# A planned attention-plus-MLP kernel: a new order for the first batch, filler matmuls, one burst of key sums, free choice of buffer slots, and 15 squares on ScalarE

## The chip, the cores and the metric

The kernel runs on one core of a Trainium2 chip. The metric is the device time in microseconds (us). The span that the profile shows is from the first to the last instruction. A run over 1.5% above the fastest of the same kernel is called slow. A ratio is the mean time of one kernel's fast runs over that of the other's from the same rounds, so it is not quite the ratio of the medians that are quoted.

## The reference

```python
def phi(x):                                   # r = 8, so phi has 64 features
    a = einsum('rd,bhsd->bhsr', S1, x)
    b = einsum('rd,bhsd->bhsr', S2, x)
    return einsum('bhsi,bhsj->bhsij', a, b).reshape(..., 64)
q_p, k_p = phi(q), phi(k)                     # batch 4, heads 4, seq 1088, head_dim 32
kv  = einsum('bhsf,bhsd->bhfd', k_p, v)
z   = sum(k_p, axis=2)
x   = einsum('bhsf,bhfd->bhsd', q_p, kv) / (einsum('bhsf,bhf->bhs', q_p, z) + 1e-6)
x   = x.transpose(0, 2, 1, 3).reshape(4352, 128)
out = relu(x @ w_in)**2 @ w_out               # w_in 128 x 2048, w_out 2048 x 128
```

## The kernel before

The program first collects all operations with a planned duration on an engine, their dependencies and a priority, and then `Plan.run` lists them out in order of a simulated time. What the planner decides is the order of instructions on each engine and the slot of each buffer; each engine runs its list in order, and semaphores do the waiting. A batch has a **key** stage (k is transposed, projected to kab, transposed to ab; VectorE forms the 64 products kp; PE sums kv and z). A **unit** of 512 tokens has a query stage (qT, a sketch of 32 matmuls, a ScalarE copy bs, a VectorE product qp, den, its reciprocal, num, xT) and a **MoE** stage of eight tiles, each: two h matmuls, a relu on ScalarE, a square on VectorE, two o matmuls.

Buffers come back in the order in which they were taken:

```python
    for buf in op.take:                       # Plan.ready
        used, bufs = self.used[buf.pool], self.pools[buf.pool][3]
        if len(used) >= bufs:
            for d in used[len(used) - bufs].readers:
                ...
                t = max(t, d.end)
```

The loads of a batch go out as k, v, q, with q in one piece; the weights follow once batch 0's k is there:

```python
    k_ops = ...; v_ops = ...                  # k in two pieces, v in six
    q_op = dma("SP", lambda e: e.dma_start(out=qst.tile, in_=qb), deps=deps, prio=prio, take=[qst])
...
    nc.gpsimd.tensor_copy(gate, loaded[0][0].tile[:, 2 * C8 - 1 : 2 * C8])
    nc.gpsimd.dma_start(out=w_in_sb, in_=...)
    nc.gpsimd.dma_start(out=w_out_sb, in_=...)
```

A MoE tile, with the choice of the squaring engine (the list is empty before the change):

```python
    a2: nc.scalar.activation(rl.tile[:, :, :R], h.tile[:, :, :R], ACTF.Relu)
    alts = {"DVE": ... eng.tensor_mul(g.tile, rl.tile, rl.tile)}
    if i in SQ_ACT:                           # SQ_ACT = ()
        alts = {"ACT": ... eng.activation(g.tile, rl.tile, ACTF.Square)}
```

PSUM holds a ring of three two-bank slots (`ring`, for h, kab, the two sketch halves, the turned key sums, den and num), one bank for o and one for kv.

Of the kernel before, what the change touches and what calls it, by code (L numbers as in the profile page):

```python
# [36 lines left out]
class Plan:  # L37
# [3 lines left out]
    def __init__(self, pools):  # L41
        self.pools = pools
        self.ops = []
        self.used = {name: [] for name in pools}
# [9 lines left out]
    def ready(self, op):  # L54
        t = 0.0
        for d in op.deps:
            if d.end is None:
                return None
            t = max(t, d.end)
        for d in op.after:  # L60
            if d.issued is None:
                return None
            t = max(t, d.issued)
        for buf in op.take:
            used, bufs = self.used[buf.pool], self.pools[buf.pool][3]
            if len(used) >= bufs:
                for d in used[len(used) - bufs].readers:
                    if d.end is None:
                        return None
                    t = max(t, d.end)  # L70
        return t

    def run(self):
        free, mode, left, log = {}, {}, list(self.ops), []
        while left:
            best = {}
            for op in left:
                t = self.ready(op)
                if t is None:
                    continue  # L80
                for eng, (busy, lat, fn) in op.alts.items():
                    at = max(t, free.get(eng, 0.0))
                    best.setdefault(eng, []).append((at, op))
            assert best, "no operation is ready"
            eng = min(best, key=lambda e: min(a for a, _ in best[e]))
# [5 lines left out]
            busy, lat, fn = op.alts[eng]  # L91
            if op.mode is not None:
                if mode.get(eng, op.mode) != op.mode:
                    at += MODE_SWITCH
                mode[eng] = op.mode
            free[eng] = at + busy
            op.issued, op.end = at + busy, at + lat
            for buf in op.take:
                pool, shape, dtype, _ = self.pools[buf.pool]
                buf.tile = pool.tile(shape, dtype, tag=buf.pool, name=buf.name)  # L100
                self.used[buf.pool].append(buf)
# [6 lines left out]
SLACK = 0.05  # L108
MODE_SWITCH = 0.1
WARM = 12  # L110
KP_POOL = ()
SQ_ACT = ()
TOGETHER = True
K_LEAD = 18.0
Q_LEAD = 2.0
Q_END = 0.0
# [3 lines left out]
def kernel(  # L120
# [26 lines left out]
    def pool(name, shape, bufs, dtype=F32, space=None):  # L147
        if space is None:
            p = ctx.enter_context(tc.tile_pool(name=name, bufs=bufs))
        else:  # L150
            p = ctx.enter_context(tc.tile_pool(name=name, bufs=bufs, space=space))
# [5 lines left out]
    assert LEFT == 2  # L157

# [59 lines left out]
    def load(b, prio, deps=(), first="SP"):  # L218
# [6 lines left out]
        for i, (c0, c1) in enumerate(((0, 2 * C8), (2 * C8, S))):  # L225
            k_ops.append(dma(
                ("SP", first)[i],
# [3 lines left out]
                deps=deps, after=k_ops[:1], prio=prio, take=[kst] if i == 0 else [],  # L231
            ))
        v_ops = []
        for c in range(4):
# [6 lines left out]
                deps=deps, after=v_ops[:1], prio=prio, take=[vt] if c == 0 else [],  # L241
            ))
        for c in range(LEFT):
# [6 lines left out]
                deps=deps, after=v_ops[:1], prio=prio,  # L250
            ))
        q_op = dma(
            "SP", lambda e: e.dma_start(out=qst.tile, in_=qb),
            deps=deps, prio=prio, take=[qst],
        )
        loaded[b] = (kst, k_ops, vt, v_ops, qst, q_op)

    load(0, -90.0, first="ACT")
# [11 lines left out]
    w_op = plan.add("POOL", 3.0, 8.0, weights, deps=loaded[0][1], prio=-80.0)  # L270

    def warm():
        ps = Buf("o", "warm_ps")
        for n in range(WARM):
            plan.add(
                "PE", 0.43, 0.6,
                lambda: nc.tensor.matmul(  # L277
                    ps.tile, zeros[:, :128], zeros, start=True, stop=True
                ),
                prio=-100.0, take=[ps] if n == 0 else [], last=[ps], mode="full",  # L280
            )

    warm()

    def sketches():
# [17 lines left out]
        plan.add("SP", 0.0, 3.5, lambda: None, prio=-99.0)], prio=-95.0)  # L303
# [25 lines left out]
    def keys(b, prios):  # L329
        kst, k_ops, vt, v_ops, _, _ = loaded[b]  # L330
        kT, ab, kv, ps = Buf("kT", "kT"), Buf("ab", "ab"), Buf("kv", "kv_ps"), Buf("ring", "kab_ps")
        p = lambda x: prios[0] + x * (prios[1] - prios[0])
        tr = []
        for i, (c0, c1) in enumerate(((0, 2 * C8), (2 * C8, S))):
# [5 lines left out]
                deps=[k_ops[i]], after=tr[:1], prio=p(0.05 * i), take=[kT] if i == 0 else [], last=[kst],  # L340
# [4 lines left out]
        def project():  # L345
# [19 lines left out]
        pr = plan.add("PE", 1.0, 1.25, project, deps=tr + [sk_op], prio=p(0.1),  # L365
# [7 lines left out]
            deps=[pr], prio=p(0.15), take=[ab], last=[ps],  # L373
# [7 lines left out]
            deps=[pr], after=[main], prio=p(0.16), last=[ps],  # L381
        )

        def sums():
            nc.tensor.matmul(
                kv.tile[:, : F + H * r], zeros[:, :128], zeros[:, : F + H * r],
                start=True, stop=False, skip_group_check=True,
            )
            for t in range(T8 + 1):
# [10 lines left out]
        last = plan.add("PE", 0.6, 0.8, sums, deps=[main, tail], prio=p(0.2),  # L400
                        take=[kv], last=[ab], mode="k")
        zsum = last
        steps = [last]
        for x, (t0, t1) in enumerate(((0, 4), (4, T8), (T8, T8 + 1))):
# [4 lines left out]
            def product(eng, t0=t0, t1=t1, P=P, n=n, kp=kp):  # L409
# [8 lines left out]

            alts = {"DVE": ((1.12, 1.25) if n > 1 else (0.33, 0.45)) + (
                lambda product=product: product(nc.vector),)}  # L420
            if (b, x) in KP_POOL:
                alts = {"POOL": ((2.4, 2.6) if n > 1 else (0.8, 0.9)) + (
                    lambda product=product: product(nc.gpsimd),)}
            pd = plan.either(alts, deps=[main, tail], prio=p(0.25 + 0.2 * x),
                             take=[kp], last=[ab])

            def accumulate(t0=t0, t1=t1, P=P, kp=kp):
                for t in range(t0, t1):
                    for h in range(H):
# [9 lines left out]
            last = plan.add("PE", 0.12 * n, 0.12 * n + 0.25, accumulate,  # L439
                            deps=[pd] + v_ops, after=[last], prio=p(0.3 + 0.2 * x),  # L440
                            last=[kp, vt], mode="k")
            steps.append(last)
        kvT, zd, st = Buf("kvT", "kvT"), Buf("zd", "zd"), Buf("ring", "st_ps")
# [9 lines left out]
            deps=[zsum, mk_op], prio=p(0.76), take=[zd], last=[kv],  # L453
# [6 lines left out]
            deps=steps, prio=p(0.75), take=[kvT], last=[kv],  # L460
        )

        def turn():
            nc.tensor.matmul(
                st.tile[:, 1, : H * r],
                spread.rearrange("p c i j -> p (c i j)"),
                zd.tile.rearrange("p h j -> p (h j)"),
                start=True,
                stop=True,
            )  # L470
            nc.tensor.transpose(
                st.tile[:, 0, :128], kvT.tile.rearrange("p c f -> p (c f)"), ident
            )

        tn = plan.add("PE", 0.4, 0.6, turn, deps=[c1, d1], prio=p(0.8),
                      take=[st], last=[kvT, zd], mode="full")
# [4 lines left out]
                in0=st.tile[:, 1, : H * r].rearrange("p (h j) -> p h j", h=H),  # L481
# [3 lines left out]
            deps=[tn], prio=p(0.85), take=[zj], last=[st],  # L485
# [4 lines left out]
                kvs.tile[:, 0].rearrange("p h d -> p (h d)"), st.tile[:, 0, :128]  # L490
            ),
            deps=[tn], prio=p(0.85), take=[kvs], last=[st],
# [6 lines left out]
            deps=[d2], prio=p(0.9), take=[zc], last=[zj],  # L499
# [6 lines left out]
            deps=[d3, c2], prio=p(1.0), last=[zc],  # L506
        )
        state[b] = (kvs, [c2, d4])


    x_ready = {}

    def queries(u, prios):
# [4 lines left out]
        p = lambda x: prios[0] + x * (prios[1] - prios[0])  # L518
# [3 lines left out]
        while c0 < g0 + 2 * W:  # L522
# [7 lines left out]
                deps=[loaded[b][5]], after=tr[:1], prio=p(0.0), take=[qT] if not tr else [],  # L530
# [19 lines left out]
        if TOGETHER:  # L550
            op = plan.add("PE", 0.1 + 0.78 * f, 0.3 + 0.78 * f, lambda: sketch((0, 1)),
                          deps=tr + [sk_op], prio=p(0.15), take=ps, last=[qT], mode="q")
            sk = [op, op]
        else:
            sk = []
            for g in range(2):
                sk.append(plan.add(
                    "PE", 0.1 + 0.78 * f, 0.3 + 0.78 * f, lambda g=g: sketch((g,)),
                    deps=tr + [sk_op], prio=p(0.15 + 0.2 * g), take=[ps[g]], last=[qT],
                    mode="q"))  # L560
        prods = []
        for g in range(2):
# [6 lines left out]
                deps=[sk[g]], prio=p(0.2 + 0.2 * g), take=[bs], last=[ps[g]],  # L569
# [9 lines left out]
                deps=[cp], after=prods[:1], prio=p(0.3 + 0.2 * g), take=[qp] if g == 0 else [],  # L579
                last=[bs, ps[g]],  # L580
            ))
        dps, nps = Buf("ring", "den_ps"), Buf("ring", "num_ps")
        batches = sorted({g0 // S, (g0 + 2 * W - 1) // S})
        st_deps = [d for b in batches for d in state[b][1]]
        kvs_last = [state[b][0] for b in batches]

        def apply(x, to):
            for h in range(H):
                for c in range(2):
                    f0 = g0 + W * c  # L590
                    while f0 < g0 + W * c + W:
# [4 lines left out]
                            to.tile[32 * h : 32 * h + 32, c, w0 : w0 + f1 - f0],  # L596
# [7 lines left out]
        da = plan.add("PE", 0.05 + 0.42 * f, 0.28 + 0.42 * f, lambda: apply(1, dps),  # L604
                      deps=prods + st_deps, prio=p(0.55), take=[dps], last=[qp] + kvs_last,
                      mode="nd")
# [3 lines left out]
            lambda: nc.vector.transpose(dT.tile[:, :, :W], dps.tile[:, :, :W]),  # L610
            deps=[da], prio=p(0.6), take=[dT], last=[dps],
# [8 lines left out]
            deps=[t1], prio=p(0.65), take=[den], last=[dT],  # L620
# [4 lines left out]
            deps=[t2], prio=p(0.7), take=[rec], last=[den],  # L625
# [7 lines left out]
            deps=[t3], prio=p(0.75), take=[rT], last=[rec],  # L633
        )
        na = plan.add("PE", 0.05 + 0.42 * f, 0.28 + 0.42 * f, lambda: apply(0, nps),
                      deps=prods + st_deps, after=[t3], prio=p(0.8), take=[nps],
                      last=[qp] + kvs_last, mode="nd")
# [126 lines left out]
```

## Time and profile before

| | before |
|---|---|
| median time | 126.31 us (126.28 to 126.38, 3 runs) |
| the profiled run | 128.53 us, span 126.7, granted clock 0.929, slow |
| first relu begins | 26.18 us |
| first relu to end of last relu | 95.1 us |
| end of last relu to end of span | 5.4 us |

The profile's page of the kernel before: busy time by engine, and then the span in 40 slices of 3.17 us, each digit the busy share in tenths; PEclk is the granted clock of the matrix engine.

```profile
PE 110.2 (87%) x1378; PEld 50.5 (40%) x1396; DVE 105.1 (83%) x208; ACT 78.6 (62%) x99; POOL 3.3 (3%) x14
PE   6973785789999999999989979999899999999940
DVE  3445756889979999999989995999999899997940
ACT  3000313036848488589657766878898898899920
PEclk9999555557999999999999999999999999999998
```

There are two regimes. In the first nine slices no engine stays full, and the clock is at half in slices 5 to 9; from there on PE and VectorE (DVE) are near 9 everywhere. The windows view of the same kernel gives the numbers: us of the stretch, its length, then busy us (and instructions) of PE, PE's weight loads, DVE, ACT, POOL, then the clock, the DMA share and GB/s.

```profile
core 0: us, PE busy (x) PEld busy (x) DVE busy (x) ACT busy (x) POOL busy (x), PEclk, DMA share, GB/s
8.00:12.00 4.00, 1.17 (x37) 0.84 (x43) 2.03 (x4) 0.00 (x0) 0.08 (x1) 1.00 1.03 304
16.00:20.00 4.00, 3.45 (x50) 1.45 (x50) 1.54 (x6) 1.11 (x3) 0.00 (x0) 0.50 1.28 287
...
26.18:121.32 95.14, 91.57 (x1133) 42.41 (x1151) 89.10 (x173) 74.64 (x92) 0.00 (x0) 0.98 0.20 40
```

The timeline of the kernel before, lines from its start (start us, us, engine, line, operation, what stood before it in brackets):

```profile
10.81 0.71 DVE L527 STREAM_TRANSPOSE qT<-qst 128x512 f32<-128x512 f32 x1 [1.77 <-DMA qst<-in_q_dram]
11.44 2.64 DVE L412 TENSOR_TENSOR kp<-ab 128x1024 f32<-128x1024 f32 x3
17.12 2.01 PE L542 MATMUL qab_ps<-qT,S12q 32*64 32x256 f32 x32 [0.55 <-DVE zj L479]
25.13 0.59 PE L664 MATMUL h_ps<-xT,w_in_sb 128*128 128x512 bf16 x1 [0.91 <-DVE xT L640]
26.18 1.02 ACT L673 ACTIVATE rl<-h_ps 128x1024 bf16<-128x1024 f32 x1 [5.95 <-remote]
28.97 1.06 PE L692 MATMUL o_ps<-g,w_out_sb 128*128 128x512 bf16 x2
```

VectorE stands for q in its program order although the inputs of kp, next in its list, have been there for 1.8 us; a sketch takes 2.01 us at half clock, where later ones take 1.1. The chain of waits that ended last, by engine, and the DMA issue of w_out (KB, us to landing):

```profile
PE 53%; DVE 25%; ACT 7%; DMA 4%; issue 3%; SPq 3%; DVEq 0%; ACTq 0%
...
w_out_sb<-in_moe_w_out_dram POOLq DMA_DIRECT2D x1, 512.0 KB, 18.8
```

The w_out load was issued at 6.91 us and so landed at 25.7, three microseconds before it was used. Nothing waited for it.

### The profile page before, as it was taken

The numbers are of one execution on the slowest core, as the hardware profiler recorded it, in microseconds if no ns is written. First come the engines' busy times: TensorE is split into PE (matmuls) and PEld (weight loads), VectorE is DVE, ScalarE is ACT, GpSimd is POOL, SyncE is SP. The second block draws the span as 40 slices with busy tenths as digits, with TensorE's granted clock in tenths as the row PEclk, the third lists the DMA queues.
The fourth block names the chain that finished last, engine by engine and source line by source line (L and its number), as shares of the span: only waits on it lengthen the run. The fifth ranks groups of instructions, "written<-read, shape, count | busy, mean of one in ns | idle before, by whom it ended". The sixth has DMA issues, their size and how long they took to land.

```text
span 126.7 us, 3355 instructions
## 1 busy us (share of the span) xinstructions
PE 110.2 (87%) x1378; PEld 50.5 (40%) x1396; DVE 105.1 (83%) x208; ACT 78.6 (62%) x99; POOL 3.3 (3%) x14
## 2 busy tenths in 40 slices
PE   6973785789999999999989979999899999999940
PEld 2231541234544543534444434334445343434620
DVE  3445756889979999999989995999999899997940
ACT  3000313036848488589657766878898898899920
POOL 3050000000000000000000000000000000000000
PEclk9999555557999999999999999999999999999998
DMA  2999999950033263050003100220013050031042
GB/s 32 294 272 273 246 282 265 241 174 33 5 85 81 39 111 124 5 83 3 5 2 57 29 0 5 38 45 0 0 28 60 0 90 3 0 57 31 7 76 41
DMA packets 25871, 10.21 MB, mean 81 GB/s; under 512 B 22144, under 2 KB 24192, under 8 KB 25856
## 3 DMA queue, kind: packets, MB, share of 16 engines
q1 hardware_dynamic: 23360, 8.64, 29.6%
q0 software_dynamic: 2208, 1.05, 6.2%
q10 hardware_dynamic: 288, 0.31, 1.0%
q8 instruction: 11, 0.18, 0.6%
q14 instruction: 4, 0.03, 0.1%
HBM read 8.81 MB, written 2.23 MB: 87 GB/s over the span
## 4 chain that ended last, share of the span: by engine, by line
PE 53%; DVE 25%; ACT 7%; DMA 4%; issue 3%; SPq 3%; DVEq 0%; ACTq 0%
PE o_ps L692 17%; PE h_ps L664 16%; DVE g L682 7%; ACT rl L673 7%; PE qab_ps L542 7%; DVE kp L412 4%; DMA qst<-in_q_dram 4%; PE num_ps L595 4%; PE kv_ps L430 4%; PE den_ps L595 3%; DVE qp L573 3%; DVE qT L527 3%; DVE ot L702 2%; PE kab_ps L348 2%; SPq L237 1%
## 5 line engine op out<-in xcount | busy, mean ns | idle before, releaser
L673 ACT ACTIVATE rl<-h_ps 128x1024 bf16<-128x1024 f32 (+1 forms) x72 | 66.5, 980 | 21.8 <-PE h_ps L664 12.6
L682 DVE TENSOR_TENSOR g<-rl 128x1024 bf16<-128x1024 bf16 (+1 forms) x72 | 44.8, 642 | 3.3 <-ACT rl L673 3.1
L692 PE MATMUL o_ps<-g,w_out_sb 128*128 128x512 bf16 (+1 forms) x137 | 37.4, 371 | 1.9 <-DVE g L682 1.2
L664 PE MATMUL h_ps<-xT,w_in_sb 128*128 128x512 bf16 (+1 forms) x133 | 37.3, 373 | 1.8 <-DVE xT L640 0.9
L664 PEld LDWEIGHTS <-w_in_sb 128*128 128x128 bf16 x144 | 12.9, 98 | 18.6 <-issue 6.8
L692 PEld LDWEIGHTS <-w_out_sb 128*128 128x128 bf16 x144 | 13.1, 98 | 17.6 <-issue 7.7
L566 ACT COPY bs<-qab_ps 128x512 f32<-128x512 f32 (+1 forms) x18 | 9.2, 565 | 14.8 <-PE qab_ps L542 14.7
L542 PE MATMUL qab_ps<-qT,S12q 32*64 32x256 f32 (+1 forms) x288 | 12.4, 405 | 3.5 <-DVE qT L527 2.1
L573 DVE TENSOR_TENSOR qp<-qab_ps,bs 128x512 f32<-128x512 f32 (+1 forms) x18 | 11.3, 650 | 1.0 <-ACT bs L566 0.8
L412 DVE TENSOR_TENSOR kp<-ab 128x1024 f32<-128x1024 f32 (+1 forms) x12 | 10.8, 921 | 0.0
L542 PEld LDWEIGHTS qab_ps<-qT,S12q 32*64 32x64 f32 x288 | 6.2, 139 | 8.4 <-DVE qT L527 2.2
L595 PE MATMUL den_ps<-qp,kvs 64*32 64x256 f32 (+3 forms) x168 | 7.3, 391 | 1.7 <-DVE den L615 1.5
L610 DVE STREAM_TRANSPOSE dT<-den_ps 128x512 f32<-128x512 f32 (+1 forms) x9 | 6.1, 675 | 2.7 <-PE den_ps L595 2.7
L527 DVE STREAM_TRANSPOSE qT<-qst 128x512 f32<-128x512 f32 (+7 forms) x12 | 6.4, 533 | 2.0 <-DMA qst<-in_q_dram 1.8
L430 PE MATMUL kv_ps<-kp,vt 128*32 128x64 f32 (+1 forms) x288 | 7.2, 238 | 0.8 <-DVE kp L412 0.3
L430 PEld LDWEIGHTS kv_ps<-kp,vt 128*32 128x32 f32 (+1 forms) x288 | 5.0, 117 | 5.4 <-issue 2.1
L337 DVE STREAM_TRANSPOSE kT<-kst 128x512 f32<-128x512 f32 (+1 forms) x8 | 5.7, 728 | 1.6 <-DMA kst<-in_k_dram 1.6
L595 PE MATMUL num_ps<-qp,kvs 64*32 64x256 f32 (+3 forms) x168 | 6.9, 369 | 0.0
L702 DVE STREAM_TRANSPOSE ot<-o_ps 128x512 f32<-128x512 f32 (+1 forms) x9 | 6.1, 683 | 0.8 <-PE o_ps L692 0.8
L640 DVE TENSOR_TENSOR xT<-num_ps,rT 128x512 bf16<-128x512 f32 (+1 forms) x9 | 5.8, 647 | 0.6 <-PE num_ps L595 0.6
L277 PE MATMUL warm_ps<-zeros 128*128 128x512 bf16 x12 | 5.2, 623 | 1.2 <-DVE zeros L190 1.2
L629 DVE STREAM_TRANSPOSE rT<-rec 128x512 f32<-128x512 f32 (+1 forms) x9 | 6.1, 674 | 0.1
(45 smaller groups left out, 46.8 us busy)
## 6 DMA issues: line engine op xcount, KB each, us to landing
qst<-in_q_dram SPq DMA_DIRECT2D x4, 544.0 KB, 5.9
vt<-in_v_dram SPq DMA_DIRECT2D x16, 128.0 KB, 5.3
out_dram<-ot SPq DMA_DIRECT2D x20, 64.0 KB, 2.0
kst<-in_k_dram SPq DMA_DIRECT2D x4, 256.0 KB, 5.0
kst<-in_k_dram SPq DMA_DIRECT2D x3, 288.0 KB, 6.2
w_in_sb<-in_moe_w_in_dram POOLq DMA_DIRECT2D x1, 512.0 KB, 8.9
w_out_sb<-in_moe_w_out_dram POOLq DMA_DIRECT2D x1, 512.0 KB, 18.8
kst<-in_k_dram ACTq DMA_DIRECT2D x1, 288.0 KB, 3.2
```

Of the source, the lines that this page charges most:

```text
L412: eng.tensor_tensor(out=kp.tile[:P, :n].rearrange("p t h i j -> p (t h) i j"), in0=a[:, :, :, None].to_broadcast([P, n * H, r, r]), in1=bb ...
L430: nc.tensor.matmul(kv.tile[32 * h : 32 * h + 32, :F], vt.tile[:P, h, t, :], kp.tile[:P, t - t0, h].rearrange("p i j -> p (i j)"), start=False,
L527: lambda c0=c0, b=b, s0=s0, n=n: nc.vector.transpose(qT.tile[:, c0 - g0 : c0 - g0 + n], loaded[b][4].tile[:, s0 : s0 + n]),
L542: nc.tensor.matmul(ps[g].tile[F * c : F * c + F, e, 256 * s : 256 * s + W], S12q[32 * h : 32 * h + 32, s].rearrange("p i j -> p (i j)"), q ...
L566: lambda g=g, bs=bs: nc.scalar.copy(bs.tile[:, :, :W], ps[g].tile[:, :, 256 : 256 + W]),
L573: lambda g=g, bs=bs: nc.vector.tensor_tensor(out=qp.tile[:, 2 * g : 2 * g + 2, :W], in0=ps[g].tile[:, :, :W], in1=bs.tile[:, :, :W], op=AL ...
L595: nc.tensor.matmul(to.tile[32 * h : 32 * h + 32, c, w0 : w0 + f1 - f0], state[b][0].tile[F * c : F * c + F, x, h, :], qp.tile[F * c : F * ...
L664: nc.tensor.matmul(h.tile[:, e, :R], w_in_sb[:, 2 * cp + e, :], xT[:, c0 : c0 + R], start=True, stop=True,)
L673: lambda h=h, rl=rl: nc.scalar.activation(rl.tile[:, :, :R], h.tile[:, :, :R], ACTF.Relu),
L682: eng.tensor_mul(g.tile[:, :, :R], rl.tile[:, :, :R], rl.tile[:, :, :R])
L692: nc.tensor.matmul(o.tile[:, :R], w_out_sb[:, ct, :], g.tile[:, e, :R], start=(ct == 0), stop=(ct == CT - 1),)
L702: lambda: nc.vector.transpose(ot.tile[:, :R], o.tile[:, :R]),
```

## The change

The intent: shorten the latency chain of the first batch, keep PE from ever idling before the first h matmul, take work from VectorE, and let the planner use whichever slot is free. The diff, cut to its core:

```diff
@@ buffers: any free slot, the earliest first
-        self.used = {name: [] for name in pools}
+        self.used = {name: [None] * pools[name][3] for name in pools}
+    def times(self, name):
+        for i, buf in enumerate(self.used[name]):
+            ends = [d.end for d in buf.readers] if buf else [0.0]
+            if all(e is not None for e in ends):
+                found.append((max(ends, default=0.0), i))
+        return sorted(found)
@@ planned idle time of PE before the first h matmul is filled with warm matmuls
+            if self.filler and eng == self.filler[0]:
+                step, work, kind = self.filler[1:]
+                while at - free[eng] > step:
+                    work()
+                    ...
-WARM = 12
-SQ_ACT = ()
+WARM_AT = 1.3
+KP_FIRST = ((0, 4, "DVE"), (4, 7, "DVE"), (7, 8, "POOL"), (8, 9, "POOL"))
+SQ_ACT = (1, 4, 5, 6, 8, 10, 12, 14, 21, 24, 27, 28, 29, 37, 46)
+FIRST_K = {"kT": -141.88, "project": 24.06, "ab": -91.07, ...}   # a priority per step
+FIRST_Q = {"qT": -94.36, "sketch": -6.11, "bs": -108.84, ...}
+K_STEPS = ...; Q_STEPS = ...
@@ q in two pieces, the first at k's priority, before v
-        q_op = dma("SP", lambda e: e.dma_start(out=qst.tile, in_=qb), ...)
+        for i, (c0, c1) in enumerate(((0, 512), (512, S))):
+            q_ops.append(dma(("SP", "SP")[i],
+                lambda e, c0=c0, c1=c1: e.dma_start(out=qst.tile[:, c0:c1], in_=qb[:, c0:c1]),
+                deps=deps, after=q_ops[:1], prio=prio + (0.0, 0.02)[i], ...))
@@ batches 1 to 3: the sums and all key accumulations as one piece of PE work
+        joint = b > 0
+            zsum = last = plan.add(
+                "PE", 1.4, 1.65, lambda: [fn() for fn in [sums] + bursts], ...)
@@ den needs z alone, num needs kv alone; unit 1's sketch follows num of unit 0
-                      deps=prods + st_deps, ...
+                          deps=prods + z_deps, ...
+        if u == 0:
+            x_hold.append(na)
@@ the last outputs go out on two queues
-                    "SP",
+                    "ACT" if c0 + R == N_TOK and i % 2 else "SP",
```

Not in the cut: the turned key sums now lie in the bank of kv, so they no longer take a slot of the ring.

## The prediction

> **What bounds the kernel now.** Two stretches.
>
> *Start, 0 to 29 us.* The first relu begins at 26.2 us, the first o_ps matmul at 29.0 (timeline). Until then PE is half idle: 1.17 of 4 us busy in 8–12, 2.46 in 20–24; the granted clock is 0.50 from 16 to 28 us (windows). The chain of waits is one of latencies: a 544 KB q load landing at 10.8 us; VectorE, in program order, waits for it before the key products (11.4); the key sums; unit 1's sketch at half clock (2.01 us instead of 1.1) before den of unit 0; and so on, to xT at 25.0.
>
> *Stream, 29 to 122 us.* PE shows about 96% busy, VectorE 94%, ScalarE 79% (windows). PE's share overstates: 0.43 us a matmul pair, 1.1 a sketch and 0.59 each den/num sum to some 81 us of 93. VectorE (squares 0.60 us back to back) is the tightest, with ring slots given back in order costing PE the rest.
>
> **What the change does.**
> - 15 squares go from VectorE (about -9.6 us) to ScalarE, where a relu of that size takes 0.97 us back to back: an estimated +14.3 us. From the first relu on ScalarE's work becomes about 90 us, VectorE's 78, PE's 81. ScalarE is the new limit. First to last relu was 95.1 us, so at most 5 us can be gained there; I expect 2 to 3 (93 us), as three nearly equal engines never interlock perfectly.
> - First batch: q is split, its first half goes before v (lands near 7 us instead of 10.8); two key tiles go to GpSimd; products start at 9 rather than 11.4 us; den no longer waits for kv; unit 1's sketch waits for num of unit 0; fillers keep PE busy. Costed from trace durations: key sums near 12.5, den near 13, xT near 16, first relu near 17.5 us instead of 26.2.
> - Fillers are planned at 0.22 us, but the warm matmuls ran 0.43 us apart until 6.4 us. PE may reach kab 2 us late, and a lag is not recovered where every gap is filled.
> - w_out landed at 25.7 us: weight loads and the loads of batches 1 and 2 share saturated DMA (240–300 GB/s to 25 us). The Trainium skill's page "DMA: Bandwidth & Descriptors", section "Queues, rings and completion order", says engines round-robin between queues by packet; the trace agrees (16–24 us: 1295 weight packets, 1324 others). The change hardly alters this; half-size q packets help a little: w_out near 23–25 us. I expect PE to stand at the first o_ps for some microseconds, eating half of the start's gain and letting the clock drop again.
> - One key burst, freer slots: fewer PE gaps, under 1 us a batch. Output queues at the end: 0.5 us.
>
> **Sum.** 17.5 + 93 + 5 (tail) = 115.5 without the w_out stall, about 119 with it fully paid. I say 116.5 us, range 111 to 121.
>
> **Right if:** first relu at 16–19 us; granted clock near 1.0 from 8 us except around a w_out wait; PE waiting on the w_out DMA at the first o_ps; ScalarE over 92% busy from 25 to 70 us, VectorE near 85%.
>
> **Wrong if:** w_out lands early, or squares on ScalarE are cheaper (faster); filler lag pushes the first relu past 21 us, or relu queues behind squares so PE lacks h tiles (slower).
>
> Chances: faster by over 2% 0.93, within 2% 0.05, slower 0.02.

## The result, and the profile after

The median time is 119.56 us (119.04 to 120.69, 4 runs) against 126.34 before; the ratio of the fast runs is 0.946 (95% interval 0.939 to 0.954). In a later control of five rounds the ratio was 0.954 (0.945 to 0.963). The profiled run is fast, 119.37 us.

| | before (slow run) | after (fast run) |
|---|---|---|
| first relu begins | 26.18 us | 18.13 us |
| first relu to end of last relu | 95.1 us | 94.7 us |
| from there to the end | 5.4 us | 4.7 us |
| span | 126.7 us | 117.6 us |

The only profile of the kernel before is of a run 2.2 us above its median. A fast run of a kernel that has the same instructions in the same order up to the first relu (the experiment `before_squares`) has its first relu at 24.46 us:

```profile
24.46 1.02 ACT L673 ACTIVATE rl<-h_ps 128x1024 bf16<-128x1024 f32 x1 [5.95 <-PE h_ps L664]
```

So the like-for-like gain is about 6.3 us at the start, next to nothing in the long stretch, and some 0.7 us at the end; together near the measured 6.8.

The page of the kernel after, the same lines:

```profile
PE 105.5 (90%) x1397; PEld 49.5 (42%) x1416; DVE 96.3 (82%) x192; ACT 90.9 (77%) x114; POOL 5.6 (5%) x16
PE   5999996599899899999989899999999999999950
DVE  3389679879799997997979669997995999887960
ACT  3103119798789998799986998999999998799930
PEclk9999999999999999999999999999999999999999
```

The half-clock digits are gone. In the windows, the stretch between first and last relu has kept its length, but its filling changed: VectorE 89.1 to 83.5, ScalarE 74.6 to 87.0.

```profile
8.00:12.00 4.00, 3.84 (x92) 2.28 (x93) 3.95 (x7) 1.07 (x2) 2.24 (x2) 1.00 1.07 242
16.00:20.00 4.00, 2.91 (x61) 1.20 (x54) 2.99 (x6) 2.83 (x4) 0.00 (x0) 1.00 1.50 240
...
18.13:112.86 94.73, 89.04 (x1150) 41.51 (x1166) 83.51 (x162) 87.03 (x108) 0.00 (x0) 1.00 0.29 62
```

The timeline of the kernel after, where the start turns into the stream:

```profile
8.82 1.20 DVE L492 TENSOR_TENSOR kp_239<-ab_236 128x1024 f32<-128x1024 f32 x1
17.07 0.39 PE L779 MATMUL ring_386<-xT,w_in_sb 128*128 128x512 bf16 x1
18.13 1.04 ACT L789 ACTIVATE rl_397<-ring_386 128x1024 bf16<-128x1024 f32 x1
19.21 0.69 DVE L798 TENSOR_TENSOR g_416<-rl_397 128x1024 bf16<-128x1024 bf16 x1
21.86 0.11 PEld L808 LDWEIGHTS <-w_out_sb 128*128 128x128 bf16 x2 [2.02 <-DMA w_out_sb<-in_moe_w_out_dram]
```

The products begin at 8.8 us instead of 11.4, and the first square is done at 19.9, but the o matmul that needs it starts at 21.9: now the load of w_out is waited for, 2.02 us by the weight load of PE; the matmuls themselves stood for 1.53 us. The view names VectorE for that gap, but the weight load just before it names the DMA. The chain by engine, and the DMA issue of w_out:

```profile
PE 54%; ACT 26%; DVE 8%; issue 8%; ACTq 0%; DVEq 0%
...
w_out_sb<-in_moe_w_out_dram POOLq DMA_DIRECT2D x1, 512.0 KB, 15.0
```

VectorE and ScalarE have changed places in the chain, 25% and 7% before, 8% and 26% after.

### The profile page after: what moved, and what is told of

The parts are those of the page before. It is cut to its first block, busy times and chain, and to the rows that moved or that the text cites. A ratio compares the mean times of both kernels' runs of the same rounds, so it can differ in the third digit from the quotient of the medians.

```text
span 117.6 us, 3394 instructions
## 1 busy us (share of the span) xinstructions
PE 105.5 (90%) x1397; PEld 49.5 (42%) x1416; DVE 96.3 (82%) x192; ACT 90.9 (77%) x114; POOL 5.6 (5%) x16
## 3 DMA queue, kind: packets, MB, share of 16 engines
q0 software_dynamic: 2208, 1.05, 6.7%
## 4 chain that ended last, share of the span: by engine, by line
PE 54%; ACT 26%; DVE 8%; issue 8%; ACTq 0%; DVEq 0%
PE o_158 L353 7%; PE o_1540 L808 3%; PE o_1269 L808 3%; PE o_1401 L808 3%; PE o_425 L808 2%; PE o_1033 L808 2%; PE o_699 L808 2%; PE kv_243 L506 1%; PE kv_1119 L506 1%; PE kv_766 L506 1%; PE o_1786 L808 1%; DVE kT_431 L415 1%; ACT g_960 L796 1%; ACT g_752 L796 1%; PE ring_1044 L426 1%
## 5 line engine op out<-in xcount | busy, mean ns | idle before, releaser
L353 PE MATMUL o_158<-zeros 128*128 128x512 bf16 x30 | 8.7, 443 | 1.4 <-DVE zeros L259 1.2
L353 PEld LDWEIGHTS <-zeros 128*128 128x128 bf16 x32 | 3.4, 114 | 5.3 <-issue 2.2
L667 ACT COPY bs_254<-ring_218 128x512 f32<-128x512 f32 x1 | 0.6, 586 | 5.7 <-PE ring_219 L643 5.7
L415 DVE STREAM_TRANSPOSE kT_179<-kst_162 128x512 f32<-128x512 f32 (+1 forms) x2 | 1.4, 724 | 1.4 <-DMA kst_162<-in_k_dram 1.4
L667 ACT COPY bs_389<-ring_363 128x512 f32<-128x512 f32 x1 | 0.6, 586 | 2.5 <-PE ring_364 L643 2.5
L789 ACT ACTIVATE rl_1079<-ring_1071 128x1024 bf16<-128x1024 f32 x1 | 1.0, 1025 | 1.3 <-PE ring_1071 L779 1.3
L492 POOL TENSOR_TENSOR kp_241<-ab_236 128x256 f32<-128x256 f32 x1 | 1.7, 1658 | 0.9 <-DVE ab_236 L447 0.9
L789 ACT ACTIVATE rl_865<-ring_858 128x1024 bf16<-128x1024 f32 x1 | 1.0, 1024 | 0.8 <-PE ring_858 L779 0.8
L789 ACT ACTIVATE rl_442<-ring_428 128x1024 bf16<-128x1024 f32 x1 | 1.0, 1024 | 0.7 <-PE ring_428 L779 0.7
L722 DVE STREAM_TRANSPOSE dT_335<-ring_325 128x512 f32<-128x512 f32 x1 | 0.7, 716 | 1.0 <-PE ring_325 L700 1.0
L798 DVE TENSOR_TENSOR g_466<-rl_442 128x1024 bf16<-128x1024 bf16 x1 | 0.7, 693 | 1.0 <-ACT rl_442 L789 1.0
L426 PE MATMUL ring_1044<-kT_815,S12k 128*32 128x256 f32 x16 | 1.1, 385 | 0.4 <-ACT rl_1031 L789 0.4
L415 DVE STREAM_TRANSPOSE kT_815<-kst_606 128x512 f32<-128x512 f32 (+1 forms) x2 | 1.4, 710 | 0.0
L674 DVE TENSOR_TENSOR qp_1503<-ring_1472,bs_1497 128x512 f32<-128x512 f32 x1 | 0.7, 692 | 0.8 <-ACT bs_1497 L667 0.8
L674 DVE TENSOR_TENSOR qp_394<-ring_363,bs_389 128x512 f32<-128x512 f32 x1 | 0.7, 692 | 0.8 <-ACT bs_389 L667 0.8
```

The costliest lines, as they stand in the source:

```text
L353: nc.tensor.matmul(warm_ps.tile, zeros[:, :128], zeros, start=True, stop=True)
L415: lambda c0=c0, c1=c1: nc.vector.transpose(kT.tile[:, c0:c1], kst.tile[:, c0:c1]),
L426: nc.tensor.matmul(ps.tile[32 * c : 32 * c + 32, 0, C8 * s : C8 * s + C8], S12k[:, s, :], kT.tile[:, C8 * c : C8 * c + C8], start=True, st ...
L492: eng.tensor_tensor(out=kp.tile[:P, :n].rearrange("p t h i j -> p (t h) i j"), in0=a[:, :, :, None].to_broadcast([P, n * H, r, r]), in1=bb ...
L667: lambda g=g, bs=bs: nc.scalar.copy(bs.tile[:, :, :W], ps[g].tile[:, :, 256 : 256 + W]),
L674: lambda g=g, bs=bs: nc.vector.tensor_tensor(out=qp.tile[:, 2 * g : 2 * g + 2, :W], in0=ps[g].tile[:, :, :W], in1=bs.tile[:, :, :W], op=AL ...
```

## The experiments

Twelve kernels in three calls; the kernels of a call share one chip and the runs of the kernel before. "Stretch" is the time from the start of the first relu to the end of the last, read from the profiled run of each kernel; "(slow)" marks a profile of a slow run. The fast runs of the kernel before had means of 126.0, 125.5 and 126.3 us in the three calls, so a difference of under about 1 us between kernels of different calls settles nothing. (The ratio of `after_12_warm` does not rest on the two runs of its mean: 119.6 over 126.0 would be 0.949, and 0.959 stands for a mean of about 120.7 us.)

| run | fast runs, mean us | ratio to before (95%) | first relu | stretch |
|---|---|---|---|---|
| after_no_squares | 125.8 (2 of 4) | 1.000 (0.979–1.021) | 19.3 (slow) | 102.7 (slow) |
| before_squares | 128.4 (2 of 4) | 1.021 (1.003–1.039) | 24.5 | 97.1 |
| after_12_warm | 119.6 (2 of 4) | 0.959 (0.940–0.978) | 19.2 | 93.4 |
| after_whole_q | 123.8 (3 of 4) | 0.984 (0.969–0.999) | 22.5 | 93.8 |
| after_again (control) | 119.7 (4 of 7) | 0.954 (0.945–0.963) | 19.3 (slow) | 99.9 (slow) |
| after_no_wout_wait | 118.3 (6 of 6) | 0.943 (0.938–0.949) | 18.1 | 93.3 |
| after_slots_in_turn | 122.1 (4 of 6) | 0.973 (0.966–0.980) | 18.2 | 96.5 |
| after_weights_first | 118.3 (6 of 6) | 0.943 (0.938–0.949) | 18.6 | 93.3 |
| weights_first_12_warm | 117.8 (2 of 6) | 0.934 (0.924–0.944) | 19.0 (slow) | 95.2 (slow) |
| after_old_first_order | 120.7 (3 of 4) | 0.956 (0.949–0.963) | 20.1 | 93.3 |
| replanned_2 | 117.5 (6 of 6) | 0.931 (0.925–0.936) | 18.1 | 92.4 |
| replanned_3 | 118.6 (6 of 6) | 0.940 (0.935–0.946) | 18.2 | 93.5 |

### What are the squares on ScalarE worth?

`after_no_squares`:

```diff
-SQ_ACT = (1, 4, 5, 6, 8, 10, 12, 14, 21, 24, 27, 28, 29, 37, 46)
+SQ_ACT = ()
```

> The kernel after the change with all 72 squares on VectorE again (the list of squares on ScalarE is emptied, the rest stays, and the order is planned anew). Theory 1: the shorter start leaves some 4 us of VectorE work to the stretch between the first and the last relu, and the squares on ScalarE are what pays for it; without them VectorE has about 93 us of work in that stretch, which must grow from 94.7 us to 98 to 100, so the time is 123 to 125 us. Theory 2: the squares only swap one full engine for another and are worth nothing; 119 to 120.5 us. First relu near 18 us in both.

`before_squares` makes the opposite edit in the kernel before.

> The kernel before the change with only the same 15 squares put on ScalarE. Theory 1: the stretch after the first relu is bound by how the engines wait for one another in program order more than by VectorE's sum alone, so the squares alone, in an order not tuned for them, bring between -1 and +2 us: 125 to 128 us. Theory 2: VectorE's 94% is the limit and taking 9 us from it pays at once: 121 to 123 us. First relu near that of before in both.

Without the squares, the kernel after is about as slow as the kernel before (ratio 1.000, give or take 2%): by the means all of its advantage is gone, and by the interval at least half, although its start is kept. Put alone into the kernel before, they make it 2% slower, just clear of zero. The windows view of the stretch, first of `after_no_squares`, then of `before_squares`:

```profile
19.30:122.00 102.70, 92.78 (x1166) 42.10 (x1166) 92.92 (x177) 73.98 (x93) 0.00 (x0) 0.98 0.26 56
```

```profile
24.46:121.53 97.07, 92.68 (x1150) 42.51 (x1151) 81.48 (x158) 87.75 (x107) 0.00 (x0) 0.98 0.21 44
```

VectorE has 92.9 us of work in the stretch of `after_no_squares`, against 89.1 before: 3.8 us more, of which 3.4 is work that the kernel before did ahead of its first relu (15.1 us there, 11.8 here). The squares take 9.4 off again (83.5). So Theory 1 holds in its main point: the time came out a little above the 123 to 125 us that it expected. One caution: the 102.7 us come from a slow run, in which w_out landed late (at 24.1 us) and PE stood 3.1 us for it; the two fast runs were 2 to 4 us shorter, with no profile. The fast runs put the worth of the squares at 6 us (125.8 against the control's 119.7), uncertain by 2 to 3 us; from the first o matmul on, the two slow profiles with a late w_out, this one and the control's, differ by 4 us (97.4 and 93.3). A rival stands untested: priorities and the list of squares were searched together, and the edit plans anew with those priorities. An order searched for a kernel without squares on ScalarE might lose less. In the kernel before the squares are worth less than nothing: `before_squares` frees VectorE to 81.5 us and the stretch still grows, from 95.1 (a slow run) to 97.1. There, in an order not tuned for it, taking work from VectorE did not pay, whatever its 94% suggested. An expectation of "121 to 123" (Theory 2) fell, and that of 125 to 128 was still a little too good.

### Is it the fillers, the early q, or the order?

`after_12_warm` issues only the first 12 filler matmuls and leaves all orders alone:

```diff
-                    work()
+                    if self.filled < 12:
+                        work()
+                    self.filled += 1
```

> The kernel after the change with the same order of all other instructions, but only the first 12 of its filler matmuls are issued, as many as the kernel before had. Theory 1: the reordering, not the fillers, makes the start short; PE has few gaps longer than 2 us left, the clock stays mostly up, the first relu comes at 18 to 19 us and the time is 119 to 120.5 us. Theory 2: the fillers keep the clock up; without them the granted clock falls to 0.5 somewhere between 8 and 20 us, the first relu comes at 20 us or later and the time is 121 us or more.

The windows view of `after_12_warm`:

```profile
8.00:12.00 4.00, 2.52 (x85) 1.63 (x75) 4.00 (x7) 1.07 (x2) 2.24 (x2) 1.00 1.06 247
12.00:16.00 4.00, 3.23 (x73) 1.31 (x73) 2.54 (x10) 0.53 (x2) 0.00 (x0) 0.65 1.27 291
16.00:20.00 4.00, 3.56 (x43) 1.25 (x36) 2.28 (x4) 1.73 (x3) 0.00 (x0) 0.50 1.53 262
```

Each theory got half. The clock fell to 0.50 in 13 to 20 us, as Theory 2 had it, and the first relu came 1.1 us later, at 19.23. Yet the span of that run was 117.3 us, no longer than with all fillers (117.6); its four runs spread from 119.12 to 123.3 us, though. The reason is in the next link: in this run the o matmuls also began only when w_out landed, at 21.6 us.

```profile
21.60 0.60 PE L811 MATMUL o<-g,w_out_sb 128*128 128x512 bf16 x2
```

The time lost to the cold clock fell inside a wait that was there anyway.

`after_whole_q` keeps the orders on the compute engines and issues each q in one piece after v:

```diff
-                lambda e, c0=c0, c1=c1: e.dma_start(
-                    out=qst.tile[:, c0:c1], in_=qb[:, c0:c1]
-                ),
+                lambda e, c0=c0, c1=c1: c0 and e.dma_start(out=qst.tile, in_=qb),
```

> The kernel after the change with the same order on all compute engines, but each batch's q is loaded in one piece, issued where the second piece was, after v. Theory 1: the early half load of q is what lets the first chain start; undivided it lands at 10 to 11 us instead of 6.9, VectorE stands at the transpose of q in program order, and the first relu comes 3 to 4 us later (21 to 22 us); the time is 122 to 123.5 us. Theory 2: the chain over the keys is as long as that over q, so only 0 to 1 us is lost: 119.5 to 120.5 us.

```profile
22.53 2.06 ACT L787 ACTIVATE rl<-ring 128x1024 bf16<-128x1024 f32 x2
25.34 0.60 PE L806 MATMUL o<-g,w_out_sb 128*128 128x512 bf16 x2 [0.60 <-DMA w_out_sb<-in_moe_w_out_dram]
```

The first relu (the first of these lines of its timeline) comes 4.4 us later than in the kernel after; the fast runs have a mean of 123.8 us, 4.1 above the control's. Theory 1 holds: the half load of q ahead of v is the largest single piece of the shorter start.

`after_old_first_order` gives the steps of the first batch the priorities that the kernel before had, and lets unit 1's sketch go ahead of num of unit 0 (`FIRST_K`, `FIRST_Q` replaced, `hold = []`).

> The kernel after the change, with the priorities of the first batch's steps as the kernel before had them, and unit 1's sketch free to go ahead of num of unit 0. Split q, early q half, two key tiles on GpSimd, fillers and squares stay; orders planned anew. Theory 1: the early loads carry most of the shorter start and the priorities only 1 to 2 us: first relu at 19 to 20.5 us, and as w_out lands at 22 anyway the time is 119.5 to 121.5 us. Theory 2: the order is what makes the start short: first relu at 22 us or later, time 122.5 us or more.

The first relu came at 20.1 us, two later; the fast runs at 120.7 us, one above the control's mean of the call before (ratios 0.956 and 0.954, whose intervals overlap). Theory 1's numbers again, but not all of its reason: nothing waited for w_out here. It landed at 22.1 us, and the first o matmul came two microseconds after that:

```profile
24.11 1.47 PE L808 MATMUL o<-g,w_out_sb 128*128 128x512 bf16 x6
```

From there to the end of the last relu the new plan took 89.3 us, less than the kernel after (91.0). The edit plans the rest anew too, so what the order of the first steps is worth by itself stays open.

### The wait for w_out

The control is the kernel after, unaltered:

> The kernel after the change, unaltered, as a control on the chip that runs the other three of this call. Both theories: 119 to 121 us, span 1.7 to 1.8 us less; w_out lands between 21 and 24 us and PE waits 1.5 to 3 us for it at the first o matmul.

Three of its seven runs were slow, up to 125.6 us, and the profile fell on one of these. Its timeline:

```profile
25.77 1.03 PE L808 MATMUL o<-g,w_out_sb 128*128 128x512 bf16 x2 [4.32 <-DMA w_out_sb<-in_moe_w_out_dram]
```

Here w_out landed at 25.8 us. PE stood 4.3 us, the clock fell to 0.50 in 24 to 28, and the first relu was already late, at 19.25. That lateness shows the filler lag. The following lines are from the timelines of the kernel after (fast run) and of the control (slow run):

```profile
1.21 5.66 PE L353 MATMUL o_158<-zeros 128*128 128x512 bf16 x18 [1.21 <-DVE zeros L259]
6.79 1.14 PE L426 MATMUL ring_205<-kT_179,S12k 128*32 128x256 f32 x16
```

```profile
1.20 6.81 PE L353 MATMUL o<-zeros 128*128 128x512 bf16 x18 [1.20 <-DVE zeros L259]
7.94 1.07 PE L426 MATMUL ring<-kT,S12k 128*32 128x256 f32 x16
```

The same 18 fillers end 1.14 us later, because the matmuls' spacing went from 0.43 to 0.22 us only at 6.7 us instead of 4.5; the first projection starts 1.15 us later and the first relu 1.12 us later. Two runs are a comparison, not a proof, but the numbers agree. The Trainium skill, page "TensorE: Matmul & The Clock Gate", part 1, calls the gate's window free-running, with a transition that varies from run to run; the two traces agree.

`after_no_wout_wait` takes the wait away with other data (a wrong result):

```diff
-                        o.tile[:, :R], w_out_sb[:, ct, :], g.tile[:, e, :R],
+                        o.tile[:, :R], (w_in_sb if m == 0 else w_out_sb)[:, ct, :], g.tile[:, e, :R],
```

> The kernel after the change, but the second matmuls of the first 512 tokens take w_in's tile in place of w_out's (same shapes, same order; a wrong result on purpose), so nothing waits for w_out's load before some 37 us. Theory 1: the wait holds up the whole stretch that follows, and 1.5 to 2.5 us come off the control's time, that is 117 to 118.5 us. Theory 2: ScalarE has work queued and is full from there on, so the wait is made good later: less than 0.7 us off. The o matmul should then start near 20 us instead of 21.9.

```profile
20.17 0.59 PE L808 MATMUL o<-g,w_in_sb 128*128 128x512 bf16 x2
```

`after_weights_first` takes it away with right results, by holding batch 1's v until w_out is there:

```diff
-                lambda e, c=c: e.dma_start(...v of chunk c...),
+                lambda e, c=c: (
+                    nc.gpsimd.tensor_copy(vt.tile[:, 0, 0, :1], w_out_sb[:, 0, :1])
+                    if b == 1 and c == 0 else None,
+                    e.dma_start(...v of chunk c...),
+                ),
```

> The kernel after the change with the load of batch 1's v held until w_out has landed: a one-column copy from w_out's tile into v's tile on GpSimd, which the v load must then follow; all orders stay the same. By the round-robin reading, w_out then shares the DMA engines only with k and half of q of batch 1 and lands at 16 to 19 us instead of 21.8, and the wait at the first o matmul goes away. Theory 1: as without the wait, 1.5 to 2.5 us off the control. If the v and q loads, now later, hold up unit 2 or the key sums of batch 1 near 28 us, less. Theory 2: less than 0.7 us off.

The timeline of `after_weights_first`:

```profile
18.29 0.18 POOL L308 CAST vt<-w_out_sb 128x1 f32<-128x1 bf16 x1 [6.71 <-DMA w_out_sb<-in_moe_w_out_dram]
20.66 0.59 PE L812 MATMUL o<-g,w_out_sb 128*128 128x512 bf16 x2
```

w_out now lands by 18.3 us, and the o matmul no longer waits for it. Both kernels had a mean of 118.3 us where the control's fast runs had 119.7: 1.4 us, slightly less than Theory 1 said (1.5 to 2.5) and twice what Theory 2 allowed. The intervals of the ratios overlap a little; the traces are clearer. The stretch is 93.3 us in both. And five kernels have one and the same order on the compute engines: from the start of the first o matmul to the end of the last relu they took 91.0 us (after: 21.87 to 112.86), 91.1 (`after_12_warm`), 91.0 (`after_whole_q`), 91.2 (`after_no_wout_wait`) and 91.2 (`after_weights_first`), each read from a fast run. So in this order nothing of a late start is made good later, and nothing more is lost: what counts is when the first o matmul begins. And all twelve of their runs were fast, within 1.4 us of each other, where three of seven of the control were slow. I read that as the late landing making the control's slow runs, since the one slow run with a profile shows exactly this; the other two have no profile.

`weights_first_12_warm` puts the cut of the fillers on top.

> The kernel of the run weights_first (batch 1's v held until w_out has landed), but with only the first 12 filler matmuls; all orders the same. In the run with 12 fillers and the old load order, the clock fell to 0.5 from some 13 to 20 us and the first relu came 1.1 us later, yet the o matmul started no later, since w_out had not landed. Theory 1: with the wait gone the cold clock counts, and this is 0.8 to 1.5 us slower than weights_first's 118.4: 119.2 to 120 us. Theory 2: the stream absorbs it: under 0.4 us.

This one is not settled. Its six runs spread from 117.09 to 120.65 us, and the time mostly goes with the granted clock (0.994 in the fastest, 0.957 in the slowest, 0.985 at 118.58); the fast ones are only two, and by those it is no slower than with all fillers. The profile is of the slowest run, with the clock at 0.50 from 16 to 24 us. The mean over all six is 119.2 against 118.3, but that mean rests on slow runs. In that slow profile the first o matmul began at 22.2 us instead of 20.7, although w_out had landed by 18.0; whether the fast runs had the cold clock too is not known. What can be said is that the times spread over 3.6 us here and over 1.0 us with all fillers (on another chip); that the fillers make the time shorter is open.

### Free choice of slots

`after_slots_in_turn` keeps everything but takes slots of each pool in turn, and plans anew:

```diff
-        for i, buf in enumerate(self.used[name]):
+        n, p = len(self.used[name]), self.turn.get(name, 0)
+        for i in [(p + k) % n for k in range(n)]:      # oldest first, later ones only after it
...
+        self.turn[buf.pool] = (i + 1) % len(self.used[buf.pool])
```

> The kernel after the change, but the slots of every pool are given back in turn, oldest first, as before the change, and the order is planned anew under that rule. Theory 1: free choice of slots shortens the gaps in which PE waits for a ring slot: in turn costs 2 us or more (121.5 us and above). Theory 2: it is worth little on the chip, under 1 us, because the waits that end last are for data, not for slots.

The fast runs have a mean of 122.1 us, 2.4 above the control. The windows view of its stretch:

```profile
18.19:114.68 96.49, 90.78 (x1166) 41.41 (x1166) 84.21 (x162) 87.42 (x108) 0.00 (x0) 1.00 0.29 61
```

The same work on all engines takes 96.5 us instead of 94.7 (this run also waited 2.1 us for w_out, as the kernel after did). Theory 1 holds, with one reserve: the priorities were searched under the free choice, so an order searched for slots in turn might lose less than 2.4 us.

### A version that beats both

The planner's PE costs were below what the trace of the kernel after shows: a sketch occupies PE 1.0 us (planned 0.88), a key burst 1.85 (1.4), the projection 1.15 (1.0), den or num 0.59 (0.47). With these costs, w_out planned at 18.6 us, and the load order of `after_weights_first`, I searched priorities and the list of squares again by the planner's own end time, which promised about 3.5 us less.

> A try at a better kernel: batch 1's v held until w_out has landed, the planner's PE costs set to what the trace of after shows (sketch 1.0, key burst 1.85, project 1.15, den and num 0.59, 0.16 for a switch of kind), w_out planned to land at 18.6 us, and priorities and squares searched again by the planner's own end time; 9 squares on ScalarE. Theory 1: the stream loses to the order in which engines wait for each other, and the planner's PE costs were too small, so a plan with the measured ones gains most of the 3.5 us that it shows: 114.5 to 116.5 us. Theory 2: the plan is over-fitted to a model that the chip doesn't follow: 117.5 to 120 us.

> As replanned_2 with another outcome of the same search: 11 squares on ScalarE, nine of them in the first 16 tiles, and queries planned further ahead. Theory 1: 114.5 to 116.5 us. Theory 2: 117.5 to 120 us.

Both gave the right results. `replanned_2`, with nine squares on ScalarE, has a median of 117.44 us and a ratio to before of 0.931; it is the fastest kernel, about 1 us below `after_weights_first` (0.943). They were run at other times. `replanned_3` has 118.43, no better. Of the 3.5 us that the planner promised, about one arrived once and none the other time, so Theory 1 fell: `replanned_2` lies at the lower edge of what Theory 2 said, `replanned_3` inside it. The stretch of `replanned_2`:

```profile
18.14:110.51 92.37, 88.45 (x1151) 42.08 (x1166) 85.96 (x168) 81.89 (x102) 0.19 (x1) 1.00 0.31 69
```

With six squares fewer on ScalarE, the two engines stand at 86.0 and 81.9 us instead of 83.5 and 87.0. The order differs too, so the number of squares is not tested by itself here. What keeps 92 us of stretch above 88 us of PE's shown busy time is open.

## Why the prediction was right or wrong, point by point

The predicted time, 116.5 us (111 to 121), holds the measured 119.56; the forecast gain was 9.8 us and the measured one 6.8.

- **The start: right.** "First relu near 17.5 us instead of 26.2": 18.13. Of the parts costed, the early half of q carries the most (4.4 us of first relu when undone), the priorities 2.0, the fillers 1.1; they overlap and do not add up. The two key tiles on GpSimd and den's independence of kv were not undone by themselves. "Instead of 26.2" was a reading from a slow run; a fast one stands near 24.5.
- **Squares: mechanism half right.** I estimated 14.3 us of ScalarE work for the 15 squares and about 90 us from the first relu on; ScalarE had 87.0. The Trainium skill, page "ScalarE: Activation LUTs", section "What ACT_TABLE_LOAD costs", gives 186 ns + 0.833 ns per element for immediate scale and bias, with an overlap of 93 ns back to back, which makes 0.95 us for 1024 elements by my estimate (single ones took 1.02 to 1.07 us here, which fits that form); the trace has 0.94 from the start of one square (35.79 us) to that of the next relu. Yet ScalarE's busy time grew by only 12.4 us (74.6 to 87.0), 0.83 a square. A likely reason is that other instructions now run back to back too, and overlap: relus follow one another after 0.91 us (33.98, 34.88, 35.79), not 0.97, which I had taken from a pair in the chain of waits (1.94 us for two) that includes the second one's full length. VectorE's work was undersized: 78 us said, 83.5 measured. "ScalarE over 92% busy from 25 to 70 us, VectorE near 85%" became 90% and 88%, and the chain turned from VectorE to ScalarE as said. That ScalarE is the limit is not shown: the stretch is 7.7 us longer than its work.
- **Why the stretch did not shrink: the wait, which I had allowed for elsewhere.** I forecast 93 us; it measured 94.7, and without the w_out wait that lies inside it 93.3, the forecast number. That this fits so well is partly luck: the 2 to 3 us of gain were a guess below an upper bound, and the work behind it was off both ways, since I treated the stretch as fixed work from which squares are taken, while the shorter start hands some 3.4 us of VectorE's work to it. That this work lengthened the stretch is not shown.
- **The w_out wait: right in kind, too large.** I said it would land at 23 to 25 us and eat half of the start's gain. In the fast profile it landed at 21.8, PE's weight load waited 2.0 us, and taking the wait away gained 1.4. In a slow run it landed at 25.8 and the clock did fall again, as predicted. The round-robin reading is not shown. Holding back v did bring the landing to 18.3 us, but any sharing of the DMA engines would do that; and the even count that I took for agreement (1295 to 1324 from 16 to 24 us) is a sum of uneven parts: from 18 to 20 us it was 615 weight packets to 198 others, from 22 to 24 us 84 to 541. What sets the landing is a short tail. In the kernel after, all but 74 of the 2208 weight packets (queue q0) had started by 19 us; these last 3% took until 21.8, while the other loads (q1) had the engines:

```profile
q1 hardware_dynamic: 613, 1.01, 100.2%
q0 software_dynamic: 74, 0.02, 6.3%
```

This is the DMA view from 19 to 21.9 us. In the control the last 16 weight packets, beside 778 others, took from 22 to 25.8 us. Why this tail is 4 us longer in one run than in another is open.
- **Filler lag: present, in some runs.** None in the fast profile (the projection began at 6.79, right as the transposed k was ready), 1.15 us in the control's.
- **"One key burst, freer slots: fewer PE gaps, under 1 us a batch": right for the slots.** Undone, they cost 2.4 us, which is 0.6 us for each of the four batches. Neither the burst nor the ring slots that the key sums no longer take were tested by themselves.
- **The step that failed: time from span.** I summed the span (115.5 to 119, measured 117.6) and wrote it down as the time. The time is about 1.8 us longer than the span; the page of the kernel before (span 126.7, median time 126.31) hid that, because it shows a slow run of 128.53. That one slip is some 1.9 of the 3.1 us by which the centre was off; the rest is the start (18.1 for 17.5) and the stretch (94.7 for 93 and the 1 us that I had allowed for the wait), less 0.3 us at the end.

## What to carry to other kernels

When a start is shortened, ask what was quietly finishing in its shadow: here a weight load that had 3 us to spare became the next wait, and some 3.4 us of vector work moved into the stream. In this plan the new start paid only together with the squares, which made room there. A busy share of 94% does not say that relieving the engine pays; undo or do the relief alone and measure, since the same 15 squares were worth some 4 to 6 us in one order and cost 2% in another, neither of them searched anew for the edit. The skill's rule of thumb, page "ScalarE: Activation LUTs", section "Rules for kernel authors", gives relu and multiplication to VectorE because it is faster per element; here VectorE did a square in about 0.6 us back to back and ScalarE in 0.94, and in the order searched for it, moving some to the slower engine paid all the same.

## What the Trainium skill lacked or had wrong

- "TensorE: Matmul & The Clock Gate", its table "Why this matters for your kernels": no PE-idle gaps over about 3 us is not enough to keep the clock. In `after_12_warm` the clock fell to half at about 13.2 us, though the longest idle time of PE from 8 us on was 1.2 us (before the matmuls at 12.28). (Further up, the page does tell of a kernel with short, frequent idle times whose clock went up and down; the row of the table leaves that out.) What decides it is open. It is not the busy share of 4 us alone: PE had been busy 2.5 of the 4 us from 8 to 12 there, and 2.5 of the 4 us from 20 to 24 in the kernel after, where the clock stayed at 1.00.
- The same page has the first microseconds at half clock, and the traces agree: the matmuls' spacing was 0.43 us until 4.5 us (6.7 in another run), against 0.22 afterwards. The profile's clock row shows 1.00 for them; the page warns only in general that clock events in a trace can be unreliable. Here the row does not fit the spacing before its first change.
- The same page gives the transition as varying by 0.5 us either way from run to run; here the spacing changed 3.3 us after the first filler matmul in one run and 5.5 us after it in another of the same kernel. In another place the page has 6 to 14 slow matmuls in runs of one kernel; by an estimate from the spacing there were about 8 and 13 here, so that range fits and the first does not.
- I found no page that says how far apart the landings of one and the same load can be on a shared, saturated set of DMA engines: w_out took 15.0 us in one run and 18.9 in another of the same kernel, the difference lying in the last 3% of its packets. ("DMA: Bandwidth & Descriptors" would be the place.)
- I found no page that gives the distance between the device time and the profile's span from first to last instruction; it was 1.8 us here (119.37 against 117.6), and 2.1 as the mean over the runs of `replanned_3`. ("Runtime: NRT & Kernel Launch" would be the place; the gap that it gives is of another kind, with the profile's total as the longer one.)
